# Loading the value rows of the first two bands by image row instead of by key tile

## The chip, the cores and the metric

The kernel runs on one core of a Trainium2 chip. TensorE does the matmuls, VectorE and ScalarE copy and scale what it leaves in PSUM, GpSimd copies small pieces and issues DMAs, and SyncE only issues DMAs. All DMAs, whoever issues them, are carried by the same 16 DMA engines. The metric is the time of one execution on the device in microseconds (us), lower is better. In profile lines KB is 1024 bytes.

## The reference

Neighbourhood attention over an image of 224 x 224 pixels with 192 channels, one head, window 7 x 7, dilation 2:

```python
qkv = x @ wqkv                      # q, k, v of 192 channels each
r0 = jnp.clip(ir - 6, 0, H - 1 - 12)    # first row of a pixel's window, same for columns
ri = r0[:, None] + jnp.arange(7) * 2
...
logits = jnp.einsum('bnc,bnkc->bnk', qf, kn) * C ** (-0.5)
p = softmax(logits, axis=-1)
o = jnp.einsum('bnk,bnkc->bnc', p, vn) @ wo
```

Every pixel attends to 49 pixels of its own row parity and, apart from the image's edges, of its own column parity.

## The kernel before, in words

The image is cut by parity. Two neighbouring pixels of a row are taken as one slot of 384 channels (`xp`), so a row has S = 112 slots. A *band* is 16 image rows; `rc` is the row parity, and a band has BR = 8 rows of each. There are NJ = 14 bands. The kernel never forms q, k and v: it folds the weights (`AW` holds the product of the query and key weights, `WP` that of value and output weights) and works on x itself.

The work runs in 28 *steps*, one for each row parity and band, in the order of `seq`: (0,0), (0,1), (1,0), (0,2), (1,1) and so on, where the first number is rc. A step has T = 7 groups t of score matmuls (`s_group`, lines 399 and 400), each followed by an exponential (line 403). Between the groups, TensorE makes the folded queries of the next step (`g_piece`, lines 343 and 351), the products of the probabilities with the value rows (`y_unit`, line 418), which ScalarE or VectorE copy out (line 424), and the output projection of the step before (`o_mm`, line 436), which VectorE divides by the row sums (lines 440 and 451). All engines run the order that is written out in the code; nothing is rescheduled.

x comes into SBUF in two layouts:

- `xt`, channels on partitions, by DMA transposes of four image rows (`load_xt`, line 91), all on SyncE's queue. Four such parts make a band. Queries, keys and the edge pieces (`edge_item`, line 287) come from it. The pool holds four bands.
- `XN[rc]` (`xn` in the profile), the value rows: 128 partitions, 64 for an even and 64 for an odd band. A *key tile* n of a band is 8 rows x 8 slots, that is 64 keys on 64 partitions (partition 8 * row + slot) with 384 channels each. There are NK = 14 tiles side by side in the free dimension, XP = 448 elements apart; the first 64 elements of each tile are constants.

`load_xn` (line 96) loads value rows by key tile: one DMA brings 8 rows x 8 slots x 768 bytes. `DOWN` lists the tiles from 13 to 0. For each column parity, `y_unit` takes the right part of the image first (tiles 7 to 13), then the left (tiles 0 to 7).

Steps 0 to 3 use the value rows of bands 0 and 1: step 0 those of band 0 with rc = 0 (64 partitions alone, `st.first`), step 1 bands 0 and 1 with rc = 0, step 2 bands 0 and 1 with rc = 1. Before the change they are loaded like this:

- SyncE's queue: the transposes of bands 0 and 1, then 7 tiles of (0,1), the transposes of band 2, and 5 tiles of (1,1). In step 1 it gets the transposes of band 3, and from step 2 on two tiles of each new band, two transposes per step, and stores.
- GpSimd: constants (iota), then a copy (`gate`, line 199) that waits for the third transpose of band 0, then all 14 tiles of (0,0). In step 0 it makes the edge copies of (0,0) (lines 322 and 323), which wait for VectorE, and then loads the remaining 30 tiles of (0,1), (1,0) and (1,1). From step 2 on it loads the other 12 tiles of each new band, after the y matmuls that last read their place.

Each DMA signals its landing on a semaphore. There are 8 for the DMAs of GpSimd and 8 for those of SyncE and ScalarE, used in turn, so a DMA waits at its issue until the one eight places before it has landed. TensorE's weight load of a value tile waits for the DMAs that wrote that tile, once.

Of the kernel before, what the change touches and what calls it, by code (L numbers as in the profile page):

```python
# [16 lines left out]
BR = 8  # L17
KC = 8
QW = KC + HALO
NEG = -30000.0  # L20
XP = 448
# [6 lines left out]
def kernel(  # L28
# [7 lines left out]
    nc = tc.nc  # L36
# [4 lines left out]
    NK = S // KC  # L41
    SR = H // 2
    scale = float(C) ** -0.5
    xp = x[0].rearrange("h (j two) c -> h j (two c)", two=2)
# [20 lines left out]
    XN = [const.tile([128, NK * XP + 64], BF, name=f"xn{rc}") for rc in range(2)]  # L65
# [19 lines left out]
    def load_xt(b, part):  # L85
        if not 0 <= b < NJ:
            return
        if b not in xt:
            xt[b] = xt_pool.tile([128, 3, 16, S], BF, name=f"xt{b}", tag="xt")
        r = 4 * part  # L90
        nc.sync.dma_start_transpose(out=xt[b][:, :, r:r + 4, :].rearrange("p t r c -> p t (r c)"),  # L91
                                    in_=xp[16 * b + r:16 * b + r + 4].rearrange("r j c -> (r j) c"))

    DOWN = list(range(NK - 1, -1, -1))

    def load_xn(eng, rc, m, tiles):

        if not 0 <= m < NJ:
            return
        p0 = 64 * (m % 2)  # L100
        r0 = 16 * m + rc
        for n in tiles:
            eng.dma_start(out=XN[rc][p0:p0 + 64, XP * n + 64:XP * (n + 1)],  # L103
                          in_=xp[r0:r0 + 15:2, KC * n:KC * (n + 1), :])

    nc.scalar.dma_start(out=wqk[:], in_=wqkv[:, 0:2 * C].rearrange("(a p) c -> p a c", p=CH))
    nc.scalar.dma_start(out=wv[:], in_=wqkv[:, 2 * C:3 * C].rearrange("(a p) c -> p a c", p=CH))
    nc.scalar.dma_start(out=wo_lo[:], in_=wo[0:128, :])
# [2 lines left out]
        load_xt(0, part)  # L111
    for part in range(4):
        load_xt(1, part)
    load_xn(nc.sync, 0, 1, DOWN[:7])
    for part in range(4):
        load_xt(2, part)
    load_xn(nc.sync, 1, 1, DOWN[:5])


    i_id = const.tile([128, 128], I32, name="i_id")  # L120
# [63 lines left out]
    def masks(eng, gi, ccs=(0, 1)):  # L184
        for cc in ccs:
            g = GB[gorder[gi] + (cc,)]
            eng.tensor_copy(out=g[CROW[cc]], in_=cmE[CROW[cc]])
            eng.tensor_copy(out=g[RROW[cc]], in_=rm[RROW[cc], gi, :].unsqueeze(1).to_broadcast([32, S, BR]))
# [8 lines left out]

    gate = const.tile([1, 1], BF, name="gate")
    nc.gpsimd.tensor_copy(out=gate[:], in_=xt[0][0:1, 0, 8, 0:1])
    load_xn(nc.gpsimd, 0, 0, DOWN)  # L200


    def filler(n):
# [30 lines left out]
    for reg in (LO, HI, OLO, OHI):  # L234
        c0, cn, p0 = reg
# [290 lines left out]
    for si, st in enumerate(steps):  # L526
        rc, j = st.rc, st.j
        prev = steps[si - 1] if si else None
        nxt = steps[si + 1] if si + 1 < len(steps) else None
        st.ysb = [work.tile([128, 2, NO, 128], BF, name=f"ysb{cc}", tag=f"ysb{cc}", bufs=2) for cc in range(2)]  # L530

        for (cc, h, ts) in yplan:
            for kt in range(2):
                pend.append((si * T + ts[kt] + (si == 0), st, cc, h, kt))
        up = None if si < 2 else (prev.rc, prev.j + 1 + prev.rc)
        if up:
            key_copy(*up, 0, nc.vector.tensor_copy, nc.vector.tensor_copy)
        for t in range(T):
            s_group(st, t)
            if t == (6 if si == 1 else 3) and rc == 0 and 2 <= j + 1 < NJ:  # L540
                edge_item(j + 1)
            if si == 0:
                if t == 0:
                    rest()
                    g_piece(0, 0, 2)
                    edge_item(0)
                    edge_copies(0, 0, nc.gpsimd)
                    load_xn(nc.gpsimd, 0, 1, DOWN[7:])
                    load_xn(nc.gpsimd, 1, 0, DOWN[:7])
                    load_xn(nc.gpsimd, 1, 1, DOWN[5:7])  # L550
                    load_xn(nc.gpsimd, 1, 0, DOWN[7:])
                    load_xn(nc.gpsimd, 1, 1, DOWN[7:])
                elif t == 1:
                    fold_wo()
                    masks(nc.vector, 2)
                    for cc in range(2):
                        onehots(nc.vector, cc, 1)
                        key_copy(1, 0, cc, nc.vector.tensor_copy, nc.vector.tensor_copy)
                elif t < 5:
                    g_piece(nxt.rc, nxt.j, t - 2)  # L560
                elif t == 5:
                    edge_item(1)
                    edge_copies(nxt.rc, nxt.j, nc.vector)
            elif t < 3 and nxt is not None:
                g_piece(nxt.rc, nxt.j, t)
            if prev is not None:
                tp_ = t - (3 if nxt is not None else 2)
                if 0 <= tp_ < 4:
                    o_out(*o_mm(prev, PIECES[tp_]))
            run_y(si * T + t)  # L570
            if t == (0 if si > 2 else 2) and si > 0 and nxt is not None:
                edge_copies(nxt.rc, nxt.j, nc.gpsimd if si > 1 else nc.vector)
            if up and t == 0:
                load_xn(nc.sync, *up, (12, 11))
                load_xn(nc.gpsimd, *up, (10, 9, 8))
            elif up and t == 1:
                load_xn(nc.gpsimd, *up, (13, 7, 6, 5, 4, 3, 2, 1, 0))
            if nxt is None and t == 4:
                store(prev, [nc.sync, nc.gpsimd], parts=(1, 2))
            if nxt is None and t == 6:  # L580
                first = o_mm(st, (0, 1, 2, 3), (0,))
            if t == 5 and up:
                key_copy(*up, 1, nc.scalar.copy, nc.vector.tensor_copy)

            if si == 1 and t in (0, 2, 4, 5):
                load_xt(3, (0, 2, 4, 5).index(t))
            elif si > 1 and t in (1, 4):
                load_xt(j + (4 if rc else 2), 2 * (rc == 0) + (t == 4))
            if si == 0 and t in (4, 5):
                key_copy(0, 1, t - 4, nc.vector.tensor_copy, nc.vector.tensor_copy)  # L590
            if si == 1:
                if t == 1:
                    grp_copy(nc.scalar.copy, 1)
                if t in (3, 5):
                    key_copy(1, 1, (t - 3) // 2, (nc.vector.tensor_copy, nc.scalar.copy)[(t - 3) // 2], nc.vector.tensor_copy)
            if si > 1 and held and t in (1, 2, 3, 5, 6):
                (nc.sync if t in (2, 5) else nc.gpsimd).dma_start(**held.pop(0))
            if t == 2 and si in (1, 2, 3, 8):
                masks(nc.vector, {1: 1, 2: 4, 3: 3, 8: 5}[si])
        if prev is not None:  # L600
            if si == 1:
                store(prev, None, later=held)
            elif nxt is not None:
                store(prev, [nc.sync])
            else:
                store(prev, [nc.sync, nc.gpsimd], parts=(0, 3), cols=(0, NO))
# [63 lines left out]
```

## Time and profile before

| | |
|---|---|
| three timed runs | 325.12, 325.93, 331.63 us; median 325.93 |
| the profiled execution, its own time | 326.44 us |
| its span, first to last instruction | 324.7 us |
| busy share of the span | TensorE 96%, its weight loads 83%, VectorE 83%, ScalarE 77%, GpSimd 67% |
| moved by DMA | 58.98 MB, 182 GB/s on average |
| granted TensorE clock, mean | 0.991 |
| value loads issued by GpSimd in the whole run | 332 |
| value loads issued by SyncE in the whole run | 60 |

How to read it: a matmul's busy time contains the depth of its pipeline, so a TensorE that is busy in nearly all of a stretch may still have room, and the waits say more than the busy share. A DMA's issue is one event on the issuing engine and its landing another; the profile gives the time between them for GpSimd's DMAs alone. SyncE's queue is shown by the issues alone. The slices of the page and the stretches of the other views count from the first instruction.

### The profile page before, as it was taken

The page shows a single profiled execution, that of the slowest core. Times are in us where ns is not written, and L with a number is a line of the kernel's source. Part 1 is how long each engine was busy: PE and PEld are TensorE (multiplying, and loading weights), DVE is VectorE, ACT ScalarE, POOL GpSimd, SP SyncE. Part 2 cuts the span into 40 slices and gives each one's busy share as a digit, 9 for nine tenths or more (in the row PEclk, how much of TensorE's full clock was granted, in tenths as well). Part 3 has the DMA queues.
Part 4 walks back from the last instruction along what each step waited for, and adds up shares of the span by engine and source line. Part 5 has one row for each costly group of instructions (what it writes and reads, how often), then busy time and mean ns, then how long its engine had stood idle before and what let it go on. Part 6 is the DMA issues. An engine that isn't in the chain of part 4 may idle for free.

```text
span 324.7 us, 12176 instructions
## 1 busy us (share of the span) xinstructions
PE 310.8 (96%) x4948; PEld 269.8 (83%) x4948; DVE 269.0 (83%) x538; ACT 249.4 (77%) x525; POOL 217.9 (67%) x446
## 2 busy tenths in 40 slices
PE   7899899999999999999999999999999999999981
PEld 4557887998889888988899888988899888988980
DVE  7677989988988989888988898888988898887771
ACT  5558677788888787878888788878787888888652
POOL 2798677978866676785668657686567866752053
PEclk9999999999999999999999999999999999999996
DMA  9999999989989998889989999899989943644233
GB/s 163 173 182 198 179 209 191 203 213 211 144 215 223 221 183 206 210 219 190 192 199 212 210 184 181 188 224 196 169 223 221 218 117 108 172 138 120 46 108 107
DMA packets 106182, 58.98 MB, mean 182 GB/s; under 512 B 92953, under 2 KB 100155, under 8 KB 106127
## 3 DMA queue, kind: packets, MB, share of 16 engines
q1 hardware_dynamic: 88767, 40.41, 65.5%
q0 software_dynamic: 16720, 17.52, 23.1%
q8 instruction: 38, 0.62, 0.8%
q10 hardware_dynamic: 640, 0.30, 0.4%
q14 instruction: 17, 0.14, 0.2%
HBM read 19.56 MB, written 19.27 MB: 120 GB/s over the span
## 4 chain that ended last, share of the span: by engine, by line
PE 79%; DVE 11%; DMA 3%; issue 2%; SPq 2%; ACT 1%; POOL 0%; POOLq 0%; DVEq 0%; ACTq 0%
PE y L418 21%; PE po L436 17%; PE pg L343 15%; PE s_ps L399 10%; PE s_ps L400 10%; PE pg L351 4%; DVE o_sb L451 4%; DVE ysb L424 2%; DMA xt<-in_x_dram 2%; SPq L91 2%; PE pe L287 1%; DMA xn<-in_x_dram 1%; DVE rs L440 1%; DVE xb L271 1%; DVE gb L357 1%
## 5 line engine op out<-in xcount | busy, mean ns | idle before, releaser
L103 POOL DMA_DIRECT2D xn<-in_x_dram x332 | 186.9, 588 | 72.9 <-PE y L418 35.6
L403 ACT ACTIVATE p_sb<-s_ps 128x448 bf16<-128x448 f32 (+3 forms) x196 | 105.6, 539 | 19.3 <-PE s_ps L400 19.0
L418 PE MATMUL y<-p_sb,xn 128*128 128x112 bf16 (+5 forms) x1736 | 107.9, 206 | 0.8 <-DVE ysb L424 0.7
L418 PEld LDWEIGHTS <-xn 128*128 128x128 bf16 (+1 forms) x1736 | 95.1, 97 | 13.6 <-issue 6.9
L400 PE MATMUL s_ps<-gb,xb 128*128 128x112 bf16 (+4 forms) x812 | 99.0, 211 | 0.3 <-ACT gb L357 0.3
L399 PE MATMUL s_ps<-ga,xa 128*128 128x112 bf16 (+4 forms) x812 | 99.4, 211 | 0.0
L424 ACT CAST ysb<-y 128x504 bf16<-128x504 f32 (+1 forms) x140 | 73.2, 544 | 33.6 <-PE y L418 30.6
L451 DVE TENSOR_TENSOR o_sb<-po,rs 128x768 bf16<-128x768 f32 x109 | 93.6, 858 | 4.6
L436 PE MATMUL po<-WP,ysb 128*128 128x193 bf16 x770 | 82.5, 247 | 1.2 <-DVE o_sb L451 0.6
L400 PEld LDWEIGHTS <-xb 128*128 128x128 bf16 (+1 forms) x812 | 76.7, 99 | 0.0
L399 PEld LDWEIGHTS <-xa 128*128 128x128 bf16 (+1 forms) x812 | 73.3, 99 | 1.8 <-issue 1.3
L343 PE MATMUL pg<-xt,aw 128*128 128x327 bf16 (+5 forms) x420 | 68.7, 296 | 1.6 <-DVE aw L249 0.7
L436 PEld LDWEIGHTS <-ysb 128*128 128x128 bf16 x784 | 62.7, 98 | 3.0 <-ACT ysb L424 1.1
L424 DVE CAST ysb<-y 128x392 bf16<-128x392 f32 (+1 forms) x84 | 49.7, 592 | 0.4 <-PE y L418 0.2
L343 PEld LDWEIGHTS <-aw 128*128 128x128 bf16 x420 | 31.2, 100 | 14.8 <-issue 1.5
L440 DVE RECIPROCAL rs<-po 128x4 f32<-128x4 f32 x110 | 19.4, 176 | 21.3 <-PE po L436 19.7
L357 DVE CAST gb<-pg 64x872 bf16<-64x872 f32 x27 | 28.6, 1058 | 6.3 <-PE pg L351 5.5
L355 ACT CAST ga<-pg 128x872 bf16<-128x872 f32 x28 | 24.8, 886 | 9.0 <-PE pg L343 9.0
L360 DVE CAST gb<-pg 64x848 bf16<-64x848 f32 x27 | 28.2, 1044 | 0.4
L365 ACT CAST ga<-pg 128x848 bf16<-128x848 f32 x28 | 24.2, 866 | 0.6 <-PE pg L343 0.3
L269 ACT COPY xa<-xt 128x896 bf16<-128x896 bf16 x25 | 23.5, 940 | 0.0
L271 DVE COPY xb<-xt 64x896 bf16<-64x896 bf16 x56 | 22.7, 406 | 0.8
(83 smaller groups left out, 156.0 us busy)
## 6 DMA issues: line engine op xcount, KB each, us to landing
xn<-in_x_dram POOLq DMA_DIRECT2D x332, 48.0 KB, 4.5
out_dram<-o_sb SPq DMA_DIRECT2D x25, 630.0 KB
xn<-in_x_dram SPq DMA_DIRECT2D x60, 48.0 KB
xt<-in_x_dram SPq DMA_TRANSPOSE x56
out_dram<-o_sb SPq DMA_DIRECT2D x50, 9.0 KB
out_dram<-o_sb POOLq DMA_DIRECT2D x9, 78.8 KB, 2.3
out_dram<-o_sb SPq DMA_DIRECT2D x7, 78.8 KB
out_dram<-o_sb SPq DMA_DIRECT2D x25, 18.0 KB
```

What stands on the lines that cost most here:

```text
L103: eng.dma_start(out=XN[rc][p0:p0 + 64, XP * n + 64:XP * (n + 1)], in_=xp[r0:r0 + 15:2, KC * n:KC * (n + 1), :])
L271: eb(out=XB[cc][rc][d, :, k0:k0 + 64].rearrange("p n (r c) -> p r n c", c=KC), in_=t[d, 1, rc:16:2, :].rearrange(v, c=KC))
L343: nc.tensor.matmul(pg[:, a_:b_, 0:nq], lhsT=AW[w], rhs=xt[b][:, k, la:la + 2 * (b_ - a_ - 1) + 1:2, q0:q0 + nq], start=(a_ == ra if kind = ...
L357: mid(out=Bt[0][0:64, 3:S, :], in_=pg[0:64, :, 0:nq].rearrange(v))
L360: mid(out=Bt[1][64:128, HALO:S, :], in_=pg[64:128, :, 3:nq].rearrange(v))
L399: nc.tensor.matmul(o, lhsT=XA[rc][:, cc, n, 0:kn], rhs=a[:, lo:hi, :].rearrange(f), start=True, stop=False)
L400: nc.tensor.matmul(o, lhsT=XB[cc][rc][:, n, 0:kn], rhs=b_[:, lo:hi, :].rearrange(f), start=False, stop=True)
L403: nc.scalar.activation(out=p[0:kn, 0:off], in_=s_ps[0:kn, 0:off], func=ACTF.Exp)
L418: nc.tensor.matmul(y[:, BR * (a_ - h0):BR * (b_ - h0)], lhsT=XN[st.rc][kp, d:d + 128], rhs=p[kp, off + BR * (a_ - lo):off + BR * (b_ - lo) ...
L424: eng(out=o, in_=y[:, 0:BR * (h1 - h0)].rearrange("p (i n r) -> p i n r", n=NO, r=BR))
L436: nc.tensor.matmul(po[:, k, 0:C + 1], lhsT=st.ysb[cc][:, kt, n, :], rhs=WP[:, cc, kt, 0:C + 1], start=(kt == 0), stop=(kt == 1))
L451: nc.vector.tensor_tensor(out=o, in0=po[:, 0:k, 0:C], in1=rs[:, 0:k].to_broadcast([128, k, C]), op=ALU.mult)
```

## The change

A new function `load_rows` loads the value rows of one band and row parity by image row: 8 DMAs, each with the 112 slots of one row, written to 8 partitions x 14 tiles x 768 bytes. It takes the place of `load_xn` for bands 0 and 1. All 32 DMAs are issued by GpSimd, the first 8 where the 14 tiles of (0,0) were, the other 24 where the 30 tiles were. The 12 tiles that SyncE issued are gone from its queue. From band 2 on `load_xn` is used as before.

```diff
+    def load_rows(eng, rc, m):
+
+        r0, p0 = 16 * m + rc, 64 * (m % 2)
+        for i in range(BR):
+            eng.dma_start(out=XN[rc][p0 + KC * i:p0 + KC * (i + 1), 0:NK * XP].rearrange("p (n f) -> p n f", f=XP)[:, :, 64:],
+                          in_=xp[r0 + 2 * i].rearrange("(n c) f -> c n f", c=KC))
+
...
     for part in range(4):
         load_xt(1, part)
-    load_xn(nc.sync, 0, 1, DOWN[:7])
     for part in range(4):
         load_xt(2, part)
-    load_xn(nc.sync, 1, 1, DOWN[:5])
...
     nc.gpsimd.tensor_copy(out=gate[:], in_=xt[0][0:1, 0, 8, 0:1])
-    load_xn(nc.gpsimd, 0, 0, DOWN)
+    load_rows(nc.gpsimd, 0, 0)
...
                     edge_copies(0, 0, nc.gpsimd)
-                    load_xn(nc.gpsimd, 0, 1, DOWN[7:])
-                    load_xn(nc.gpsimd, 1, 0, DOWN[:7])
-                    load_xn(nc.gpsimd, 1, 1, DOWN[5:7])
-                    load_xn(nc.gpsimd, 1, 0, DOWN[7:])
-                    load_xn(nc.gpsimd, 1, 1, DOWN[7:])
+                    for rc, m in ((0, 1), (1, 0), (1, 1)):
+                        load_rows(nc.gpsimd, rc, m)
```

Since every row transfer writes to all 14 tiles, the first weight load of a step now waits for all 8 transfers of each band and parity that it reads, and the later ones of that step for none.

## The prediction

> **What bounds the kernel now.** I read the page first (span, then the chain of waits), then the table of who waited for whom, then busy time by stretches of the span, then the queues' order of time.
>
> ```profile
> span 324.7 us, 12176 instructions
> PE 79%; DVE 11%; DMA 3%; issue 2%; SPq 2%; ACT 1%; POOL 0%; POOLq 0%; DVEq 0%; ACTq 0%
> ```
> ```profile
> POOL xn L103 <- DMA xn<-in_x_dram: 25.2, 24, 2.3
> PEld L418 <- DMA xn<-in_x_dram: 0.2, 1, 0.2
> ```
> TensorE carries 79% of the chain. The value rows `xn` hold its weight loads (line 418) up once, for 0.2 us. The 25.2 us that GpSimd spends on landings is GpSimd's own time: GpSimd has 0% of the chain. So an earlier arrival of value rows can win next to nothing, and the question is whether anything arrives too late. The table by stretches (us; busy time of each engine; granted clock, share of the 16 DMA engines, GB/s) says how tight that is:
>
> ```profile
> core 0: us, PE busy (x) PEld busy (x) DVE busy (x) ACT busy (x) POOL busy (x), PEclk, DMA share, GB/s
> 0.00:14.00 14.00, 11.01 (x66) 6.28 (x67) 10.22 (x33) 7.15 (x20) 6.58 (x27) 1.00 1.02 163
> 14.00:28.00 14.00, 13.82 (x147) 8.98 (x146) 11.14 (x29) 9.38 (x23) 13.03 (x24) 1.00 1.15 191
> 28.00:41.00 13.00, 11.74 (x191) 9.88 (x187) 10.55 (x23) 9.79 (x21) 9.04 (x16) 1.00 1.24 186
> 41.00:46.00 5.00, 4.66 (x71) 3.52 (x69) 4.19 (x9) 3.56 (x8) 3.15 (x7) 1.00 1.29 206
> 74.00:84.00 10.00, 10.00 (x176) 9.08 (x175) 8.51 (x18) 8.10 (x18) 8.50 (x19) 1.00 0.89 204
> ```
> Until 46 us the DMA share is above 1 (packets overlap on the engines); in the steady part it is 0.89. The early stretch, the one that the change rearranges, is where transfers are dense: what one queue gets sooner another gets later.
>
> **What is moved.** SyncE's queue and GpSimd, in order of time (start, length, count):
>
> ```profile
> 0.74 16.04 SPq L91 DMA_TRANSPOSE xt<-in_x_dram  x8
> 16.83 5.93 SPq L103 DMA_DIRECT2D xn<-in_x_dram  x7
> 22.80 8.83 SPq L91 DMA_TRANSPOSE xt<-in_x_dram  x4
> 31.68 4.43 SPq L103 DMA_DIRECT2D xn<-in_x_dram  x5
> 36.16 9.11 SPq L91 DMA_TRANSPOSE xt<-in_x_dram  x4
> ```
> ```profile
> 9.43 6.33 POOL L103 DMA_DIRECT2D xn<-in_x_dram  x10
> 16.41 2.65 POOL L103 DMA_DIRECT2D xn<-in_x_dram  x4 [0.64 <-DMA xn<-in_x_dram]
> 19.05 0.34 POOL L322 COPY gb<-ge 64x9 bf16<-64x9 bf16 x1
> ```
> ```profile
> 20.52 7.31 POOL L103 DMA_DIRECT2D xn<-in_x_dram  x13
> ```
> ```profile
> 35.03 6.55 POOL L103 DMA_DIRECT2D xn<-in_x_dram  x11 [2.34 <-DMA xn<-in_x_dram]
> ```
> SyncE loses its 7 + 5 value loads, 5.93 + 4.43 = 10.4 us of its queue. Nothing but those loads stands between the transposes, and the instruction order shows none of the moved ones waiting for a compute engine, so the transposes of bands 2 and 3 follow the first eight directly: from 16.8 to about 16.8 + 8.83 + 9.11 = 34.7 us, not 45.3. That wins nothing by itself, since no engine waits for them in the table of waits. It puts 8 transposes of 344 KB (128 x 3 x 448 x 2 bytes) ahead of the last value rows.
>
> GpSimd issues 32 transfers instead of 44 (14 + 30), of 84 KB (86,016 bytes) instead of 48.0. What one costs it to issue:
>
> ```profile
> xn<-in_x_dram POOLq DMA_DIRECT2D x332, 48.0 KB, 4.5
> ```
> ```profile
> L103 POOL DMA_DIRECT2D xn<-in_x_dram x14: 571/612/911, 9.4 to 18.4; - x14
> DMA to landing us min/median/max: 5.3/5.5/6.6
> ```
> ```profile
> L103 POOL DMA_DIRECT2D xn<-in_x_dram x30: 551/573/716, 20.5 to 41.0; - x30
> DMA to landing us min/median/max: 3.8/5.3/7.5
> ```
> ```profile
> L489 POOL DMA_DIRECT2D out_dram<-o_sb x2: 571/580/588, 318.0 to 318.9; - x2
> ```
> A 48 KB load has 64 runs of 768 bytes, an image row 112. No row shows a load of 112 runs; the L489 stores have 120 runs (8 x 15) and took 571 and 588 ns. Bounds: 0.57 us, the price of 64 runs, and 1.0 us, 112/64 of it. I take 0.6, from the row of nearest run count. The 12 issues fewer are worth 12 x 0.57 = 6.8 us of GpSimd, which is not on the chain: nothing.
>
> **Step 0 (band 0, first parity).** The first y at 23.03 us now waits for all 8 row transfers, where it had waited for 7 of 14 tiles.
>
> ```profile
> 19.84 1.65 PE L343 MATMUL pg<-xt,aw 128*128 128x327 bf16 x6
> ```
> ```profile
> 23.03 0.47 PE L418 MATMUL y<-p_sb,xn 64*128 64x56 bf16 x7
> ```
> The eighth is issued at 9.43 + 7 x 0.6 = 13.6 us; no semaphore slot is reused before the ninth. Landing costs between 5.5 us (the row above) and 112/64 of it, 9.6: 19.1 to 23.2, against 23.03. I take about 21, no wait; at worst 0.2 us. But by then GpSimd has handed over 8 x 86 = 688 KB (thousand bytes) by 14.2 us, where before 10 loads (491 KB) were out at 15.8: some 0.2 MB more ahead of the transposes of band 1, at 191 GB/s 1.0 us. The six matmuls at 19.84 read those. They show no wait, and how much they have in hand isn't shown; the cost is between 0 and 1.0 us. Behind them on TensorE stands everything, so it would shift the rest; as the next wait swallows it, I add nothing.
>
> GpSimd's four edge copies (19.05 to 20.52, 1.5 us) are reached at 14.2 and come as soon as VectorE has their input; nothing in the table of waits was late for them. The other 24 transfers start between 14.2 + 1.5 = 15.7 and the 20.5 of before; I take the middle, 18.1.
>
> **Step 1** needs the second eight, at 35.29 us.
>
> ```profile
> 35.29 0.39 PE L418 MATMUL y<-p_sb,xn 128*128 128x56 bf16 x5
> ```
>  Issued from 18.1 to 22.9, they land by 32.5 even at 9.6 us: no wait.
>
> **Step 2** needs the last sixteen, all of them, at its first y; before, it needed half of the tiles.
>
> ```profile
> 45.77 0.46 PE L418 MATMUL y<-p_sb,xn 128*128 128x56 bf16 x7
> ```
> ```profile
> 46.48 0.83 PE L436 MATMUL po<-WP,ysb 128*128 128x193 bf16 x8
> ```
> ```profile
> 47.55 0.54 DVE L188 COPY gb<-rm 32x896 bf16<-32x896 bf16 x1
> 48.13 0.18 DVE L440 RECIPROCAL rs<-po 128x4 f32<-128x4 f32 x1
> ```
> Each transfer waits for the one eight before it, so three rounds follow one another: 18.1 + 4.8 + 3 x L, which is 39.4 us with L = 5.5 and 51.7 with L = 9.6. Between these ends I go by bytes. Sixteen transposes are 5.50 MB, the values 56 x 48.0 KB = 2.75 MB, the weights 0.29 MB: 8.55 MB, all of which is now asked for before that y. The stretches moved 14 x 163 + 14 x 191 + 13 x 186 = 7.37 MB by 41 us; the other 1.18 MB take 5.7 us at 206 GB/s or 6.3 at 186: 46.7 to 47.3. GpSimd issues its last rows late, so they are among the last to land; with the completion on top I take 48.0 to 48.9, an estimate. TensorE is there at 45.8, so it waits 2.2 to 3.1 us. Queued behind that weight load are the scores, the projection of step 1 (line 436) and the g pieces of step 3; VectorE is busy with masks until 48.1 and reads the projection then, which was done at 47.3, so 0.8 us are hidden. Sum: +1.4 to +2.3, taken at the upper end, as GpSimd's next 12 loads and edge copies also start late. After this the order is unchanged.
>
> **The clock of the matmuls.** A row of the trace decides what a longer wait would cost:
>
> ```profile
> 15.57 0.30 PE L399 MATMUL s_ps<-ga,xa 128*64 128x112 bf16 x1
> 15.67 0.30 PE L400 MATMUL s_ps<-gb,xb 128*64 128x112 bf16 x1
> ```
> ```profile
> 23.50 0.21 PE L400 MATMUL s_ps<-gb,xb 128*64 128x112 bf16 x1
> 23.55 0.21 PE L399 MATMUL s_ps<-ga,xa 128*64 128x112 bf16 x1
> ```
> The same matmuls follow each other every 0.10 us at 15.6 and every 0.05 at 23.5, while the granted clock stands at 1.00 in both stretches: TensorE starts at half rate and gets its full rate near 21.5. The Trainium skill (TensorE: Matmul & The Clock Gate, Part 1) says that an idle window of about 3.4 us brings the half rate back. My wait of up to 3.1 us stays under that, so by that rule the sum is the same; for a longer one it would add to the second rival. No run here shows a fall back to half rate.
>
> **The rivals.**
> *The rows overtake the transposes.* With 8 x 86 KB in flight instead of 8 x 48, GpSimd's queue may get a larger share of the engines and its last row land at 39 to 45 us (the lower bound, L = 5.5). Then no wait appears: 325.9. For it: landing had a minimum of 3.8 us even here. Against: the maximum was 7.5.
>
> *The narrow rows are slow (slower).* Each transfer writes 8 partitions instead of 64, all of its runs into two short groups. Suppose GpSimd's queue moves no more bytes per us than before: 30 x 48.0 KB from 20.52 to 41.58 is 68 KB per us. 24 x 84 KB then take 29.6 us from 18.1, the last is issued near 47 and lands near 52: TensorE waits 6.5 us, less 0.8 hidden, +5.7. At half rate for as long as the 6 us from 15.6 to 21.5, another 3 us are lost: +5.7 to +8.7, 332 to 335. It decides from a wait of about 7 us on. The Trainium skill (SBUF — State Buffer, Door 1: The DMA port swizzle) speaks for it: the rate goes with the number of ports that the partitions reach, 27 GB/s each, and eight neighbouring partitions reach two. By that rule an 86 KB row takes 1.6 us, 32 of them one after another 51 us, and the first y of step 2 comes near 61 us, an estimate: about +15, 341. Against it stand narrow transfers in this trace, GpSimd's stores from 15 partitions beside loads into 64, in the same stretch:
>
> ```profile
> out_dram<-o_sb POOLq DMA_DIRECT2D x9, 78.8 KB, 2.3
> ```
> ```profile
> DMA to landing us min/median/max: 5.1/5.1/5.1
> ```
> ```profile
> DMA to landing us min/median/max: 3.0/4.4/4.8
> ```
> At 50 to 63 us the stores landed in 5.1 us, the 48 KB loads (52 to 66 us) in 4.4: 1.2 times as long for 1.6 times the bytes. But they leave SBUF, the rows enter it.
>
> *A gain.* GpSimd has less to do and SyncE is free 10 us sooner. The idle time of TensorE is 0.2 us from 14 to 28, 1.3 from 28 to 41 and 0.3 from 41 to 46: at most 1.8 us, 324.1, unless more of its busy time is stretched than shows.
>
> **The numbers.** The profiled execution took 326.44 us in all, 324.7 of it span; the median of the three is 325.93, 0.5 lower. The forecast is +2.3: 328.7 against the profiled execution, 328.2 against the median. Chances: forecast 0.45; overtaking 0.21; narrow rows 0.27; gain 0.07. The range 324.8 to 335.5 holds the first two and half of the third, 0.80. Two per cent, about what a measurement of this kernel can tell from no change, is 6.5 us, so the bounds are 319.4 and 332.5. Slower by more: the narrow rows, 0.27. Faster by more: only if the gain goes past the idle time, 0.05. Within: 0.45 + 0.21 + 0.02 = 0.68.
>
> **What would show it.** In the profile after: GpSimd's 8 issues of about 0.6 us each from 9.4; transposes without a break to about 35 us on SyncE's queue; a wait of TensorE's weight loads for `xn` of 2 to 3 us between 45 and 49 us, and none worth naming at 23 and 35; landings of 6 to 9 us; from step 4 on the same steps as before, shifted. Landings over 10 us, or a wait at the first y of step 0, would make the narrow rows right; no wait at step 2 and landings under 6 us, the overtaking. An earlier end with full TensorE busy time unchanged would prove me wrong altogether.

## The result, and the profile after

| | before | after |
|---|---|---|
| median of six timed runs each, on the same chip | 326.66 us (325.12 to 331.63) | 344.06 us (341.32 to 344.74) |
| the profiled execution, its span | 324.7 us | 342.0 us |

The ratio is 1.0518, with a 95% interval of 1.0486 to 1.0551: 17.4 us slower, where +2.3 us was forecast. Ratios leave disturbed executions out; with rows to every second partition these are two of four, the profiled one among them.

The lines of after are numbered differently: the row loads are line 110, the g pieces 348 and 356 (343 and 351 before), the edge pieces 292 (287), the scores 404 and 405 (399 and 400), y 423 (418). First the page: the span, the chain by engine, and the two groups of value loads with their median time from issue to landing.

```profile
span 342.0 us, 12163 instructions
...
PE 70%; DMA 15%; DVE 7%; issue 2%; POOL 2%; SPq 1%; ACT 1%; POOLq 0%; DVEq 0%; ACTq 0%
...
xn<-in_x_dram POOLq DMA_DIRECT2D x288, 48.0 KB, 4.1
xn<-in_x_dram POOLq DMA_DIRECT2D x32, 84.0 KB, 11.1
```

TensorE's share of the chain fell from 79% to 70%, and landings rose from 3% to 15%. A row takes 11.1 us to land; the forecast had it between 5.5 and 9.6. Where the time went shows in the table of stretches (columns as before):

```profile
core 0: us, PE busy (x) PEld busy (x) DVE busy (x) ACT busy (x) POOL busy (x), PEclk, DMA share, GB/s
0.00:14.00 14.00, 11.23 (x68) 6.51 (x69) 10.72 (x35) 7.35 (x21) 6.81 (x26) 1.00 1.02 167
14.00:28.00 14.00, 7.78 (x55) 4.31 (x53) 5.77 (x16) 4.78 (x13) 7.15 (x14) 1.00 1.22 117
28.00:41.00 13.00, 12.31 (x157) 8.42 (x155) 8.22 (x16) 9.49 (x19) 5.43 (x10) 1.00 1.27 138
41.00:46.00 5.00, 5.00 (x91) 4.96 (x91) 4.65 (x13) 3.63 (x10) 1.50 (x3) 1.00 1.10 82
46.00:56.00 10.00, 5.12 (x66) 4.25 (x63) 4.56 (x12) 2.74 (x5) 3.04 (x6) 0.83 1.23 130
```

The 16 DMA engines are as busy as before (share 1.22 and 1.27, against 1.15 and 1.24), but they move 117 and 138 GB/s instead of 191 and 186. Busy engines that move less: each packet takes longer. TensorE, busy for 13.82 us of 14 to 28 before, is busy for 7.78. The table of waits says for what it waits (us in total, times, longest):

```profile
POOL xn L110 <- DMA xn<-in_x_dram: 19.2, 12, 2.3
...
PE pg L348 <- DMA xt<-in_x_dram: 6.7, 2, 6.2
...
PE pe L292 <- DMA xt<-in_x_dram: 4.9, 1, 4.9
PE y L423 <- DMA xn<-in_x_dram: 2.9, 1, 2.9
```

Two of the three waits are not for value rows but for `xt`, the transposes on SyncE's queue, whose loads the change did not touch. SyncE's queue and the first rows of GpSimd's, in order of time:

```profile
0.74 60.69 SPq L91 DMA_TRANSPOSE xt<-in_x_dram  x16
```
```profile
9.21 5.53 POOL L110 DMA_DIRECT2D xn<-in_x_dram  x8
...
17.63 1.48 POOL L110 DMA_DIRECT2D xn<-in_x_dram  x2
20.35 1.17 POOL L110 DMA_DIRECT2D xn<-in_x_dram  x2 [1.24 <-DMA xn<-in_x_dram]
23.81 1.17 POOL L110 DMA_DIRECT2D xn<-in_x_dram  x2 [2.29 <-DMA xn<-in_x_dram]
```

The 16 transposes stand without a break, as forecast, but the last is issued by 61.4 us instead of about 35: 60.69 / 16 = 3.8 us each, against 16.04 / 8 = 2.0 for the first eight of before (mean time of one issue). GpSimd's issues take 0.6 us, but from the second band on they come in ones and twos, each after the landing of the row eight places before it. The chain of waits shows this as four landings in a row (start, length, what):

```profile
9.26 4.30 POOL xn L110 x6
13.56 12.44 DMA xn<-in_x_dram
...
26.86 11.74 DMA xn<-in_x_dram
...
38.89 12.11 DMA xn<-in_x_dram
...
51.29 10.26 DMA xn<-in_x_dram
...
61.69 0.53 PE y L423 x7
```

So the first y of step 2 runs at 61.69 us, where before it ran at 45.77. Per step, from the first exponential of one to that of the next (us, worked out from the exponentials in each trace):

```
                        step 0   step 1   step 2   step 3   step 4
before                   14.57    13.04    10.96    11.18    10.47
after                    22.29    18.14    15.63    11.10    10.44
```

Steps 0, 1 and 2 lose 7.7, 5.1 and 4.7 us, 17.5 in sum, and from step 3 on nothing differs. TensorE's three waits, 6.2 + 4.9 + 2.9 = 14.0 us, are most of it.

### The profile page after: what moved, and what is told of

It is laid out like the page before. It is cut to its first block, busy times and chain, and to the rows that moved or that the text cites. A ratio compares the mean times of both kernels' runs of the same rounds, so it can differ in the third digit from the quotient of the medians.

```text
span 342.0 us, 12163 instructions
## 1 busy us (share of the span) xinstructions
PE 315.3 (92%) x4948; PEld 273.1 (80%) x4948; DVE 269.1 (79%) x538; ACT 249.7 (73%) x525; POOL 212.2 (62%) x434
## 4 chain that ended last, share of the span: by engine, by line
PE 70%; DMA 15%; DVE 7%; issue 2%; POOL 2%; SPq 1%; ACT 1%; POOLq 0%; DVEq 0%; ACTq 0%
PE y L423 19%; PE po L441 16%; DMA xn<-in_x_dram 14%; PE pg L348 13%; PE s_ps L404 9%; PE s_ps L405 9%; PE pg L356 3%; DVE o_sb L456 3%; DVE ysb L429 1%; POOL xn L110 1%; DMA xt<-in_x_dram 1%; PE pe L292 1%; SPq L91 1%; DVE rs L445 1%; DVE gb L362 1%
## 5 line engine op out<-in xcount | busy, mean ns | idle before, releaser
L103 POOL DMA_DIRECT2D xn<-in_x_dram x288 | 161.3, 585 | 73.6 <-PE y L423 49.2
L405 PE MATMUL s_ps<-gb,xb 128*128 128x112 bf16 (+4 forms) x812 | 100.5, 212 | 0.3 <-ACT gb L362 0.3
L404 PE MATMUL s_ps<-ga,xa 128*128 128x112 bf16 (+4 forms) x812 | 100.8, 213 | 0.0
L441 PE MATMUL po<-WP,ysb 128*128 128x193 bf16 x770 | 83.5, 249 | 0.9 <-DVE ysb L429 0.5
L405 PEld LDWEIGHTS <-xb 128*128 128x128 bf16 (+1 forms) x812 | 77.8, 100 | 0.0
L348 PE MATMUL pg<-xt,aw 128*128 128x327 bf16 (+5 forms) x420 | 70.0, 299 | 7.0 <-DMA xt<-in_x_dram 6.7
L404 PEld LDWEIGHTS <-xa 128*128 128x128 bf16 (+1 forms) x812 | 74.4, 100 | 1.9 <-issue 1.3
L441 PEld LDWEIGHTS <-ysb 128*128 128x128 bf16 x784 | 63.5, 98 | 2.5 <-ACT ysb L429 1.1
L360 ACT CAST ga<-pg 128x872 bf16<-128x872 f32 x28 | 24.8, 886 | 15.4 <-PE pg L348 15.4
L110 POOL DMA_DIRECT2D xn<-in_x_dram x32 | 20.2, 635 | 19.6 <-DMA xn<-in_x_dram 19.2
## 6 DMA issues: line engine op xcount, KB each, us to landing
xn<-in_x_dram POOLq DMA_DIRECT2D x32, 84.0 KB, 11.1
```

The costliest lines, as they stand in the source:

```text
L348: nc.tensor.matmul(pg[:, a_:b_, 0:nq], lhsT=AW[w], rhs=xt[b][:, k, la:la + 2 * (b_ - a_ - 1) + 1:2, q0:q0 + nq], start=(a_ == ra if kind = ...
L360: nc.scalar.copy(out=A[0][:, 3:S, :], in_=pg[:, :, 0:nq].rearrange(v))
L404: nc.tensor.matmul(o, lhsT=XA[rc][:, cc, n, 0:kn], rhs=a[:, lo:hi, :].rearrange(f), start=True, stop=False)
L405: nc.tensor.matmul(o, lhsT=XB[cc][rc][:, n, 0:kn], rhs=b_[:, lo:hi, :].rearrange(f), start=False, stop=True)
L441: nc.tensor.matmul(po[:, k, 0:C + 1], lhsT=st.ysb[cc][:, kt, n, :], rhs=WP[:, cc, kt, 0:C + 1], start=(kt == 0), stop=(kt == 1))
```

## The experiments

Each kernel is compared with the kernel before on the same chip, in runs that stand beside its own. In the diffs, minus is the changed kernel unless said otherwise. The theories: *partitions* (a transfer to few neighbouring partitions is slow, and slows what shares the DMA engines with it), *source* (the same for reading pieces 6,144 bytes apart), *bytes* (86 thousand bytes per transfer, eight in flight), *queues* (transposes that follow one another without a value load between them).

**Queues: all 56 loads by key tile, all on GpSimd.**

```diff
-    load_rows(nc.gpsimd, 0, 0)
+    load_xn(nc.gpsimd, 0, 0, DOWN)
...
-                        load_rows(nc.gpsimd, rc, m)
+                        load_xn(nc.gpsimd, rc, m, DOWN)
```

> All 56 value loads of bands 0 and 1 stay on GpSimd, as after the change, but in the old form, by key tile (48 KB, 64 partitions); SyncE's queue is as after the change, the transposes of bands 2 and 3 in one run. Theory P (the row transfers are slow because each writes only 8 neighbouring partitions, and they hold the DMA engines up for the transposes as well): 326 to 329 us, tile landings near 5 to 6 us, a transpose issue near 2 us. Theory S (each run's source lies 6144 bytes behind the last): the same, 326 to 329. Theory B (86 thousand bytes per transfer, eight in flight): the same. Theory Q (the transposes without a break, and no value load on SyncE): 340 us or more, as after the change.

Measured: 334.77 us, ratio 1.0275 (1.0213 to 1.0338). The transposes are issued by 38 us, the queues move 182 and 197 GB/s, steps 0 and 1 take 14.01 and 13.81 us (14.57 and 13.04 before): the unbroken transposes cost at most the 0.8 us of step 1. What is lost lies in step 2 (18.01 us), and it is another loss than after's. Its table of waits has TensorE wait for `xn` alone:

```profile
PEld L423 <- DMA xn<-in_x_dram: 7.4, 3, 5.9
...
PE y L423 <- DMA xn<-in_x_dram: 6.5, 2, 5.4
```

No theory had foreseen it. 56 issues at 0.57 us with eight places leave GpSimd handing over the last value tiles near 51 us. The run changes two things that can have caused this, and does not separate them: GpSimd issues the 12 tiles that SyncE's queue carried before, and the order of the tiles is another. The wait ends with tile 7 of (1,1), issued at 46.19 us and landed at 50.71. Ahead of it, from 36.70 to 41.85 us, stand seven tiles of (1,0) that step 2 needs only later; the kernel before issues these behind it. Without them tile 7 would land near 45.6 us (an estimate, 5.15 us earlier), and TensorE is there at 45.31. So the order alone can account for the first wait, and what SyncE's 12 tiles were worth is not shown.

**Partitions: every fourth of 32 instead of 8 neighbouring ones.** Bytes, runs, issues and queues stay.

```diff
-            eng.dma_start(out=XN[rc][p0 + KC * i:p0 + KC * (i + 1), 0:NK * XP].rearrange("p (n f) -> p n f", f=XP)[:, :, 64:],
+            eng.dma_start(out=XN[rc][p0 + 32 * (i // 4) + i % 4:p0 + 32 * (i // 4) + i % 4 + 29:4, 0:NK * XP].rearrange("p (n f) -> p n f", f=XP)[:, :, 64:],
```

> As after the change, one image row per transfer, but its 8 slot groups are written to every fourth partition (32 * (i // 4) + i % 4 + 4 * c for row i) instead of 8 neighbours. Same count, size, source and queue. The rows of V lie on other partitions than the keys, so the attention is computed with permuted values. Theory P: 326 to 330 us, landings back to 6 to 8 us, 180 GB/s or more from 14 to 41 us. Theories S, B and Q: 340 us or more, landings near 11 us, nothing changed.

Measured: 329.50 us, ratio 1.0102 (1.0057 to 1.0146): 3.2 us above the kernel before, so 14.2 of the 17.4 are gone. The landing of its row loads (by line: shortest, median, longest) and its stretches from 14 to 41 us:

```profile
DMA to landing us min/median/max: 4.6/7.1/8.4
```
```profile
14.00:28.00 14.00, 11.05 (x94) 6.57 (x93) 8.04 (x20) 6.97 (x17) 9.04 (x18) 0.76 1.21 182
28.00:41.00 13.00, 12.30 (x199) 10.32 (x198) 10.90 (x26) 10.56 (x24) 6.99 (x13) 1.00 1.29 209
```

Landing falls from 11.1 to 7.1 us, the queues move 182 and 209 GB/s, the transposes are issued by 43 us, and steps 1 and 2 take 13.04 and 10.68 us. Step 0 keeps 3.1 us of loss, most of it one wait of 2.6 us for a transpose of band 1.

**Source: the same 8 neighbouring partitions, read in one piece of 10,752 bytes for each.**

```diff
-                          in_=xp[r0 + 2 * i].rearrange("(n c) f -> c n f", c=KC))
+                          in_=xp[r0 + 2 * i].rearrange("(c n) f -> c n f", c=KC))
```

> As after the change, 8 neighbouring partitions per transfer, but each partition gets 14 slots that follow one another in memory (slots 14c to 14c+13) instead of every eighth slot. Same count, size and destination. The values of a key are then those of another slot. Theory P: 340 us or more, landings near 11 us. Theory S: 326 to 330 us, landings 6 to 8 us. Theories B and Q: 340 us or more.

Measured: 343.01 us, ratio 1.0516 (1.0457 to 1.0574), landing 10.5 us: as slow as after. The source is not it.

**Bytes: two key tiles at a time, 96 KB to 64 partitions, 28 transfers.**

```diff
-        for i in range(BR):
-            eng.dma_start(out=XN[rc][p0 + KC * i:p0 + KC * (i + 1), 0:NK * XP].rearrange("p (n f) -> p n f", f=XP)[:, :, 64:],
-                          in_=xp[r0 + 2 * i].rearrange("(n c) f -> c n f", c=KC))
+        for n in range(NK - 2, -1, -2):
+            eng.dma_start(out=XN[rc][p0:p0 + 64, XP * n:XP * (n + 2)].rearrange("p (n f) -> p n f", f=XP)[:, :, 64:],
+                          in_=xp[r0:r0 + 15:2, KC * n:KC * (n + 2), :].rearrange("r (c n) f -> r c (n f)", n=2))
```

> 28 transfers of 96 KB on GpSimd, two neighbouring key tiles each, written to 64 partitions; each partition's 1536 source bytes are contiguous, so half of the values are those of a neighbouring slot. SyncE's queue as after the change. Theory P: 326 to 330 us, landings 6 to 9 us. Theory B: 340 us or more, as there are more bytes in flight than in the row form. Theory S: 326 to 330. Theory Q: 340 or more.

Measured: 333.30 us, ratio 1.0215 (1.0148 to 1.0282), landing 9.4 us, 133 and 165 GB/s, steps 20.42, 14.48, 10.18 us. Between the theories: wide transfers of this size also hold the transposes up, in step 0 by 5.9 us where the narrow rows take 7.7. The number of partitions alone does not explain that.

**A middle: every second partition of 16.**

```diff
-            eng.dma_start(out=XN[rc][p0 + KC * i:p0 + KC * (i + 1), 0:NK * XP].rearrange("p (n f) -> p n f", f=XP)[:, :, 64:],
+            eng.dma_start(out=XN[rc][p0 + 16 * (i // 2) + i % 2:p0 + 16 * (i // 2) + i % 2 + 15:2, 0:NK * XP].rearrange("p (n f) -> p n f", f=XP)[:, :, 64:],
```

> The changed kernel with its 32 row loads written to every second partition of 16 instead of 8 neighbouring ones (the runs before wrote every fourth of 32: 329.5 us, landing 7.1 us; neighbours: 344.1 us, landing 11.1 us). Bytes, issues and queues are unchanged; the value rows lie on permuted partitions, so other keys' rows are summed. If the damage comes from how few partitions next to one another a transfer writes to, as a matter of degree: a landing of 8 to 9 us, the 4608-byte packets at a median of 350 to 450 ns (563 and 280 at the two ends), the DMA queues at 150 to 180 GB/s from 14 to 41 us, and 333 to 337 us. If it is only a step between touching and not touching partitions: the same as every fourth, 329 to 330 us and a landing of about 7 us.

The landing of its row loads:

```profile
DMA to landing us min/median/max: 4.2/9.3/12.4
```

That is 9.3 us, with the 4608-byte packets at 452 ns, 139 and 162 GB/s, which would make it a matter of degree. The time is less sharp: 330.50, 332.88, 337.16 and 337.28 us, ratio 1.0135 (1.0013 to 1.0256) from the first two. The profile is that of the third, in which TensorE waits 4.8 us for `xn` in step 2, so the place between the two ends is indicated, not shown.

**Eight narrow rows alone.** The kernel before, with (0,0) alone loaded by row to neighbouring partitions (minus is the kernel before).

```diff
-    load_xn(nc.gpsimd, 0, 0, DOWN)
+    load_rows(nc.gpsimd, 0, 0)
```

> The kernel before with one edit: the 14 key tile loads of (0, 0) on GpSimd become 8 row loads, each to 8 neighbouring partitions; the 12 key tile loads on SyncE and the other 30 on GpSimd stay. If eight narrow rows by themselves hold up band 1's transposes, which are then on the way: TensorE waits for transposes in step 0, which takes 19 to 23 us for 14.6, later steps take what they took or a little less, and the kernel takes 331 to 335 us. If narrow rows do harm only because the 24 others and the unbroken transposes keep the queues filled behind them: step 0 takes at most 16 us and the kernel 326 to 328 us.

Measured: 334.75 us, ratio 1.0229 (1.0148 to 1.0310). Steps: 22.80, 13.03, 10.95 us. From its table of waits (line 350 is the g piece here):

```profile
PE pg L350 <- DMA xt<-in_x_dram: 6.4, 1, 6.4
```

Eight transfers cost all of step 0's loss: TensorE waits 6.4 us for a transpose of band 1, which lands 14.6 us after its issue (8.3 in the trace of before). The value rows themselves arrive in time.

**The first band by tile, the other 24 rows to every fourth partition.** `load_rows` is that of every fourth partition, and one more line differs:

```diff
-    load_rows(nc.gpsimd, 0, 0)
+    load_xn(nc.gpsimd, 0, 0, DOWN)
```

> The changed kernel with the first eight rows, those of (0, 0), loaded as before by key tile (14 transfers on GpSimd), and the other 24 row loads written to every fourth partition; SyncE has no value load. The values of (0, 1), (1, 0) and (1, 1) lie on permuted partitions, so other keys' rows are summed. With all 32 rows on every fourth partition 3.1 us of step 0 were left over against the kernel before (17.6 us for 14.6), with TensorE waiting 5.6 us for a transpose of band 1. If that is the first eight rows running ahead of band 1's transposes: step 0 takes 14.3 to 15.0 us, the waits of step 0 for transposes go, and the kernel takes 326 to 327 us. If it is SyncE's order, with the transposes of bands 2 and 3 following those of band 1 directly: step 0 stays at 17 us or more and the time at 329 us or more.

Measured: 329.39 us, ratio 1.0042 (0.9997 to 1.0087). Step 0 takes 13.37 us and has no wait for a transpose, so what was left over above was the first eight 84 KB transfers ahead of band 1's transposes, not SyncE's order. The expected 326 to 327 us did not come, because step 1 takes 18.39 us: after 14 issues for (0,0), GpSimd reaches the rows of (0,1) at 19.87 us instead of 17.70 (all rows to every fourth partition), the last of the eight lands at 35.0 us instead of 29.2, and it is waited for, as the table of waits shows.

```profile
PE y L423 <- DMA xn<-in_x_dram: 3.5, 2, 3.2
```

**Sixteen late rows, to every fourth partition and to neighbouring ones.** The kernel before with (1,0) and (1,1) alone by row; the two kernels differ in the partitions only (minus is the kernel before).

```diff
-    load_xn(nc.sync, 1, 1, DOWN[:5])
...
-                    load_xn(nc.gpsimd, 1, 0, DOWN[:7])
-                    load_xn(nc.gpsimd, 1, 1, DOWN[5:7])
-                    load_xn(nc.gpsimd, 1, 0, DOWN[7:])
-                    load_xn(nc.gpsimd, 1, 1, DOWN[7:])
+                    load_rows(nc.gpsimd, 1, 0)
+                    load_rows(nc.gpsimd, 1, 1)
```

> The kernel before with one edit: the 28 key tile loads of (1, 0) and (1, 1), 5 of them on SyncE, become 16 row loads on GpSimd in their old place there, each to every fourth of 32 partitions; (0, 0) and (0, 1) stay by key tile. The values of (1, 0) and (1, 1) lie on permuted partitions, so other keys' rows are summed. It makes 12 issues fewer and gets the last rows in early without touching step 0. If early arrival and fewer issues are worth nothing because TensorE is the bound: steps as before within 0.3 us (14.6, 13.0, 11.0) and 326 to 328 us. If the issues or SyncE's five loads cost the kernel before something: 323 to 325 us.

> The same kernel with the 16 row loads written to 8 neighbouring partitions each, as in the changed kernel. If the harm of a narrow row lies only in holding up band 1's transposes in step 0: the same as with every fourth partition, 326 to 328 us. If late narrow rows also hold up what comes behind them (the eighth before, and the transposes of band 2): eight rows about 11 to 12 us from issue to landing, the sixteenth issued from about 36 us and in at 46 to 49 us, near the 48 us at which step 2 takes it; step 0 as before, 0 to 3 us lost in steps 1 and 2 each, and 327 to 332 us.

Measured: 327.48 us (ratio 1.0018, 0.9979 to 1.0056) and 336.87 us (1.0290, 1.0191 to 1.0390). The stretch of 28 to 41 us and the waits of TensorE, first with every fourth partition, then with neighbouring ones (line 293 is the edge piece):

```profile
28.00:41.00 13.00, 11.82 (x191) 9.91 (x187) 10.64 (x23) 9.88 (x21) 6.14 (x11) 1.00 1.26 184
```
```profile
PE y L424 <- DMA xn<-in_x_dram: 0.7, 1, 0.7
...
PE pe L293 <- DMA xt<-in_x_dram: 0.5, 1, 0.5
```
```profile
28.00:41.00 13.00, 8.53 (x137) 7.30 (x134) 9.74 (x20) 8.22 (x18) 4.25 (x8) 0.95 1.26 95
```
```profile
PE pe L293 <- DMA xt<-in_x_dram: 11.2, 1, 11.2
...
PE y L424 <- DMA xn<-in_x_dram: 0.8, 1, 0.8
```

The same bytes in the same issues at the same places: 184 GB/s or 95, a wait of 0.5 us or of 11.2, and it is again a transpose, the last of band 2, that is late (20.3 us from issue to landing). Steps 0 to 2 take 13.38, 24.59 and 12.40 us with neighbouring partitions. The second theory was right in kind and too small: it had 327 to 332 us. With every fourth partition the 12 issues fewer and the earlier rows are worth nothing, as forecast; steps 0 to 2 take 14.77, 13.04 and 11.58 us, so step 2 is 0.6 us longer than the 11.0 expected.

The two parts nearly add up to the whole: eight early narrow rows cost 334.75 - 327.09 = 7.7 us, sixteen late ones 336.87 - 327.88 = 9.0, and the change with all 32 costs 17.4. The agreement is loose: the eight rows of (0,1) are in neither run, and sixteen late rows lose 11.6 us in step 1 alone, where the change loses 5.1.

**The price of a load by itself.** The kernel before, and after its last store 8 rows to neighbouring partitions (line 626), 8 to every fourth (line 630), and 14 key tiles.

```diff
+    for i in range(BR):
+        nc.gpsimd.dma_start(out=XN[0][KC * i:KC * (i + 1), 0:NK * XP].rearrange("p (n f) -> p n f", f=XP)[:, :, 64:],
+                            in_=xp[2 * i].rearrange("(n c) f -> c n f", c=KC))
+    for i in range(BR):
+        p1 = 32 * (i // 4) + i % 4
+        nc.gpsimd.dma_start(out=XN[0][p1:p1 + 29:4, 0:NK * XP].rearrange("p (n f) -> p n f", f=XP)[:, :, 64:],
+                            in_=xp[2 * i].rearrange("(n c) f -> c n f", c=KC))
+    load_xn(nc.gpsimd, 0, 0, DOWN)
```

> The kernel before, with loads appended behind its last store, when nothing else is on the DMA queues: 8 rows of image (0, 0) to 8 neighbouring partitions each, then the same 8 rows to every fourth of 32 partitions, then its 14 key tiles, all on GpSimd's queue; nobody reads them, and they lengthen the run, so only their durations count. If the price of a narrow row is its own, its few neighbouring partitions: eight together land in 10 us or more from the first issue of theirs to the last landing behind it less the issues, their 4608-byte packets have a median over 450 ns, and rows on every fourth partition land in 5 to 7 us with packets under 300 ns. If it comes from crossing with the transposes on SyncE's queue: narrow rows land here as fast as spread ones, 5 to 7 us, and the packets of both are under 300 ns.

The two groups of rows by line: the ns of an issue (shortest, median, longest), when they were issued, and the time to landing; first neighbouring, then every fourth partition:

```profile
L626 POOL DMA_DIRECT2D xn<-in_x_dram x8: 587/588/602, 320.4 to 324.5; - x8
...
DMA to landing us min/median/max: 4.3/4.7/5.2
```
```profile
L630 POOL DMA_DIRECT2D xn<-in_x_dram x8: 587/587/590, 327.4 to 332.1; - x8
...
DMA to landing us min/median/max: 2.5/2.6/2.8
```

Both theories were partly wrong. A narrow row is dear by itself: it lands in 4.7 us against 2.6, and its 4608-byte packets (a packet is the unit in which the trace records a DMA) take 660 ns against 178, the medians of those that start from 323 us, when the last stores have landed, to 328 and from 330 to 335. But it is far from 10 us: alone, the eight land 0.71 us apart (324.67 to 329.64 us), little slower than the 0.59 us of their issue. The landing of 11 us comes only in company with the transposes. In that company the packets do not take more time than alone (564 ns, in the table below), so what is added to the landing passes outside them.

**Do the image rows of two whole tiles meet?** The last run takes 96 KB at a time too, in place of the loop over rows, but so that no two of the eight image rows of a transfer lie in the same partitions modulo 32.

```diff
+        for a, b in ((10, 14), (6, 10), (2, 6), (0, 2)):
+            for h in range(2):
+                s0 = KC * a + 4 * (b - a) * h
+                eng.dma_start(out=XN[rc][p0 + 32 * h:p0 + 32 * h + 32, XP * a:XP * b].rearrange("p (n f) -> p n f", f=XP)[:, :, 64:],
+                              in_=xp[r0:r0 + 15:2, s0:s0 + 4 * (b - a), :].rearrange("r (c n) f -> r c (n f)", c=4))
```

> The changed kernel's 32 row loads become 32 loads of mostly 96 KB (8 of them 48): 8 image rows x 4 slots x 4 (or 2) key tiles, to 32 neighbouring partitions, in which each image row has 4 partitions of its own; queues and places stay. The values lie on permuted partitions, so other keys' rows are summed. The load of two whole key tiles at a time, also 96 KB but to 64 partitions, was slow (333.3 us, landing 9.4 us, packets of 4608 bytes 468 ns), which the number of partitions does not explain. If that was the bytes of a transfer, or its runs per share: the same here or worse, 332 us or more, landing 9 us or more, the DMA queues at 130 to 165 GB/s from 14 to 41 us, TensorE waiting 4 us or more for a transpose of band 1. If it was that two shares of a transfer meet on the same group of partitions (rows 0 and 4 of a key tile lie 32 partitions apart), which cannot happen here: like the rows on every fourth partition, 328 to 330.5 us, landing 6.5 to 8 us, packets of 4608 bytes near 280 ns, 180 to 210 GB/s.

Measured: 331.42 us, ratio 1.0133 (1.0028 to 1.0239), between the two expectations, so the time does not decide. The rest is divided. The landing of the 96 KB loads (7.6 us by the page), the packets (266 ns) and the rate from 28 to 41 us are what the second theory expected; the 165 GB/s from 14 to 28 us and a wait of 4.2 us for a transpose of band 1 are what the first did:

```profile
14.00:28.00 14.00, 9.68 (x82) 5.54 (x80) 7.06 (x17) 6.31 (x16) 9.03 (x16) 0.76 1.22 165
28.00:41.00 13.00, 12.31 (x194) 9.87 (x192) 10.57 (x24) 10.29 (x22) 9.34 (x14) 1.00 1.25 194
```
```profile
PE pg L350 <- DMA xt<-in_x_dram: 4.6, 2, 4.2
```

Steps 1 and 2 take 13.03 and 10.68 us. The loss is in step 0 (18.60 us), where eight large loads (96 KB, two of them 48) cross with band 1's transposes, as with every fourth partition (17.63). So rows that do not meet help, and the size of the first loads keeps a price of its own.

The packets of GpSimd's queue with 4608 bytes, the commonest large size, from 10 to 46 us (after to 60, every second to 50), median ns, worked out from the packet records of each trace, beside the rates of the table of stretches:

```
                                  packet ns   GB/s 14-28   GB/s 28-41   time us
before (key tiles)                      204          191          186    326.66
key tiles, all on GpSimd                207          182          197    334.77
4 tiles x 4 slots, 32 partitions        266          165          194    331.42
rows, every fourth partition            280          182          209    329.50
rows, every second partition            452          139          162    330.50 to 337.28
two tiles, 64 partitions                468          133          165    333.30
rows, neighbouring, source whole        513          128          138    343.01
after (rows, neighbouring)              564          117          138    344.06
```

## Why the prediction was wrong

- *What bounds the kernel*: right. TensorE waits for nothing worth naming before, and earlier value rows win nothing: with the late rows spread, 327.48 us beside 327.88.
- *What is moved*: the order was right and its pace wrong. The transposes do follow one another, but at 3.8 us each, to 61.4 us. The prediction moved each transfer at the speed that it had in the trace of before, as if the others did not matter to it, and put the delay of the transposes behind band 1's at nothing.
- *Issue*: 0.59 us against 0.6, right, and off the path, as said.
- *Step 0*: wrong, 7.7 us against nothing added. The shape of the reasoning was right (rows ahead of band 1's transposes, read by the g pieces at 19.84 us), but its price was set by bytes at 191 GB/s: 0 to 1.0 us. The run with eight narrow rows alone shows 8.2 us in this step.
- *Step 1*: a loss of 5.1 us against none. No wait for value rows there, as said; the wait is for the transposes of band 2, which was not among the steps.
- *Step 2*: the wait for `xn` is 2.9 us, inside the forecast 2.2 to 3.1, but at 58.8 to 61.7 us instead of 46 to 48. The agreement is an accident: both sides of the wait had moved by some 13 us.
- **The step that failed** is the price of the transfer: "Between these ends I go by bytes", with 186 to 206 GB/s taken from transfers of another form. The rate was 117 and 138, and the number of bytes does not set it: with every fourth partition the same bytes in the same transfers went at 182 and 209. Left out with it were the transposes on the other queue, which those transfers held up: 11.1 us of waits where the sum had nothing.
- *The narrow rows* were the right rival with 0.27, and the prediction's own sign of it came (landings over 10 us: 11.1). It was priced too low (332 to 335), as it counted only the wait for the rows themselves. Of the 14.0 us that TensorE waits, 11.1 are for the transposes that cross with them. The rows that were held against it, stores from 15 partitions, leave SBUF; they say nothing of rows that enter it. The Trainium skill (SBUF — State Buffer, Door 1: The DMA port swizzle) gave 341 us and the first y of step 2 near 61 by the estimate in the prediction, against 344.06 and 61.69. This is in part luck: the estimate lets the rows follow one another at 1.6 us each and puts the whole loss into one wait at step 2, which took 2.9 us. In the trace up to eight rows are under way at once, to different groups of partitions. They end 1.5 us apart in company (the eighth, sixteenth, twenty-fourth and last land at 26.2, 38.6, 51.0 and 61.6 us) and 0.71 alone, so neither is the price of one row. That a full port also holds up other traffic of the engines that write to it is told by the Trainium skill of transfers between cores (DMA: Bandwidth & Descriptors, Back-pressure in remote DMA: stalled writes stall the source engine's other queues too). These runs agree with it for loads from memory: the transposes are the other queue, and eight narrow rows made one of them land after 14.6 us instead of 8.3. That ports are the cause is argued from the partitions, not shown; no record here names a port.
- *The clock*: the prediction took a wait of up to 3.1 us as too short to bring the half rate back. It came back after 2.9 us. The y and the scores right behind the wait for `xn`, in order of time, from the trace of after:

```profile
61.69 0.53 PE L423 MATMUL y<-p_sb,xn 128*128 128x56 bf16 x7 [2.92 <-DMA xn<-in_x_dram]
...
62.11 0.30 PE L405 MATMUL s_ps<-gb,xb 128*128 128x112 bf16 x1
62.20 0.30 PE L404 MATMUL s_ps<-ga,xa 128*128 128x112 bf16 x1
62.29 0.30 PE L405 MATMUL s_ps<-gb,xb 128*128 128x112 bf16 x1
```

  They follow every 0.09 us, until 65.3, then every 0.05. The clock records of the trace have half rate from 61.94 to 65.35 us and, after the wait of 4.9 us, from 51.70 to 55.11: 3.4 us each time. With rows to every fourth partition a wait of 2.55 us was enough: the scores follow every 0.05 us at 18.2 and every 0.09 from 22.5 to 26.3. The wait of 6.2 us is another case. The scores ahead of it (15.4 to 19.2 us) follow every 0.09 us too, so it brought nothing back but put off the first rise, from 21.65 us before to 31.22. At these two times the clock records of the two traces begin, and the tables count what lies ahead of them as full: the 1.00 that they show beside half rate, and on which the prediction remarked, is no measurement. Of the 17.5 us of the three steps 14.0 are waits. Two stretches of 3.4 us at half rate cost at most 1.7 us each (an estimate), so most of the other 3.5 can be this. The waits of 2.9 and 2.55 us differ from the 3.4 us of the Trainium skill (TensorE: Matmul & The Clock Gate, Part 1); the measurement decides. The trace of before has a fall back to half rate too, which the prediction missed: at 318.61 us, behind its last matmuls.

What stays open: why neighbouring partitions make the packets long. The last run fits in part with pieces of a transfer that meet on the same partitions modulo 32, but it changes the number of runs at one partition too. Nor do the traces say which of the 16 DMA engines carried a packet: that a narrow row keeps to few of them is a rival that no run here excludes.

## What to carry to other kernels

Before you merge transfers, look at how many partitions one of them writes at a time and how those lie: 84 KB to 8 neighbouring partitions took 11.1 us to land and held back the transposes of another queue, 84 KB to every fourth partition 7.1. Here the first to suffer was not the queue that was changed but another that shares the 16 DMA engines with it, so price a new transfer against what crosses with it, and read the DMA share and the GB/s together: a high share with fewer GB/s is the mark. Where a stretch is dense with transfers, a rate taken from one form of transfer is no price for another. And merging is no gain by itself: none of the merged forms tried for both bands was faster than the key tiles.

## What the runs showed that was not expected

- Eight transfers are enough: 8 rows to neighbouring partitions, issued within 5.2 us (8.84 to 13.99), made the next transposes of another queue land after 14.6 us instead of 8.3, and cost the kernel 7.7 us.
- Sixteen such rows brought all DMA queues from 184 to 95 GB/s for 13 us, while the DMA share stayed at 1.26.
- Alone on the queues the same rows landed in 4.7 us, the spread ones in 2.6, a difference of 2.1; in the kernel it was 11.1 and 7.1, a difference of 4.0. The ratio does not grow (1.8 and 1.6).
- The granted clock of the table reads 1.00 from 28 to 41 us of after, although the scores follow at half rate until 31.2: the trace's first clock record stands at 31.22 us, and what lies ahead of it counts as full. Waits of 2.9 and 2.55 us were enough for 3.4 and 4.6 us of half rate.
